# Four weighted slices in place of five plain ones for VectorE's share of the exponentials, with new scheduling constants, in an attention kernel

## The chip, the core and the metric

The kernel runs on one core of one Trainium2 chip. The metric is the device time of one execution, in microseconds (us). Each execution is marked fast or slow. A program on one core has no second core to compare with, but every execution used here is marked fast. Engines: PE is the matrix engine (TensorE), PEld its weight loads, ACT is ScalarE, DVE is VectorE, POOL is GpSimd, SP issues the DMAs.

The order of all instructions on every engine is fixed when the kernel is built: a scheduler written in Python, inside the kernel file, estimates times and places the work.

## The reference, cut to what matters

Two attentions over the same `x` (2048 tokens, width 640, 32 heads of 20) are mixed by a gate. A is full attention, with 32x2048x2048 exponentials. B is a dilated window of 8 keys, small in matmuls but large in elementwise work.

```python
scores = jnp.einsum("bhqd,bhkd->bhqk", q, k) * scale     # A: all pairs
p = _softmax(scores, axis=-1)
o = jnp.einsum("bhqk,bhkd->bhqd", p, v)
# B: keys at pos, pos-2, ..., pos-14 only
return g * a + (1 - g) * b
```

## The kernel before

A group is 512 queries of four heads. It has 64 score tiles (16 key blocks x 4 heads), each 128 keys x 512 queries in PSUM, and there are 32 groups: 2048 tiles. The scores are scaled so that 512 units are one octave.

ScalarE takes most tiles, two or three at a time:

```python
exps[s] = T("act", actc(512 * n), lambda e: e.activation(
    ebuf[s % NE][:, 0:512 * n], score[s % 2][:, 0:512 * n], ACTF.Exp, scale=LN2 / STEP), ...)
```

VectorE takes the rest in quads (one key block, four heads). A tile that it takes is called a ride. For each it moves the scores to 16-bit integers (an "eviction", `uD`). Then come the slices (`eD`), one per shift and quad. A slice computes `0.25*u + shift` as an int16 and lets PE read those bits as a bf16. That is a power of two with a straight line between octaves. The sum of several slices with different shifts smooths the line. The sum costs no addition, because PE accumulates P·V of every slice into the same bank:

```python
SHIFTS = (12001.875, 11976.375, 11952.625, 11935.625, 12034.125)
...
for k in range(K):                                   # gen_d
    T("dve", ..., lambda e, k=k, sl=sl: e.tensor_scalar(
        eD[:, sl % NS, 0:512 * n].bitcast(I16), uD[d % 2][:, 0:512 * n],
        0.25, SHIFTS[k], op0=ALU.mult, op1=ALU.add), ...)
```

The scheduler opens a quad when VectorE's backlog is small and the quad is far enough ahead of the end of its group (cuts marked):

```python
if idle < -DWAIT:                                    # VectorE too far behind
    return None
if not dopen:
    if ulock[...] or len(dquads) > cur["pv"] + 1 or ... or not (
            idle >= DIDLE2 or idle >= DIDLE and ...
            bdone[0] >= (now - BT0) / (BT1 - BT0) * BALL):    # B late: no quad
        return None
    ...  # and the quad must lie at least DTIME ahead
```

The padding (`filler`) issues matmuls that nobody reads wherever the plan leaves PE idle. At the end, the output projection of the last 512 rows (the "last fold") is prepared in `gen_prefold`; only the last group's share waits for `oN`.

## Time and profile before

| | before |
|---|---|
| time | 899.73 us median of 4 |
| ScalarE busy | 856.9 of 897.7 us |
| VectorE busy | 682.0 us |
| tiles of ScalarE / of VectorE | 1828 / 220 (55 quads) |
| exponential instructions | 726 |
| first exponential starts, last one ends | 21.3, 886.9 us |

The table of engines of the kernel before (busy time, share of the span, instructions):

```profile
span 897.7 us, 31434 instructions
PE 870.3 (97%) x13882; PEld 325.1 (36%) x13882; DVE 682.0 (76%) x1159; ACT 856.9 (95%) x760; POOL 79.2 (9%) x99
PE 75%; ACT 15%; DVE 5%; issue 3%; DMA 1%; SPq 0%; POOLq 0%; DVEq 0%; ACTq 0%; POOL 0%
```

The third line is the chain that ended last. It names PE, and so does the busy share, yet the groups of instructions argue against PE as the limit. Columns: line, engine, operation, output<-input, shapes, count | busy us, mean ns of one | idle us before them <- what ended it.

```profile
L1375 ACT ACTIVATE ebuf<-score 128x1536 bf16<-128x1536 f32 x377 | 525.4, 1477 | 7.9 <-PE score L1352 6.6 <-ACT ebuf L1375 0.3
L1375 ACT ACTIVATE ebuf<-score 128x1024 bf16<-128x1024 f32 x348 | 338.8, 1042 | 13.1 <-PE score L1352 11.1 <-PE score L487 0.3 <-PE side L844 0.2
...
L710 DVE TENSOR_SCALAR eD<-uD 128x2048 int16<-128x2048 uint16 x275 | 185.3, 703 | 20.2 <-PE obank L1410 19.6
L1365 DVE TENSOR_SCALAR uD<-score 128x512 uint16<-128x512 f32 x220 | 149.0, 687 | 57.7 <-PE score L1352 53.0 <-PE side L844 2.9
...
L1431 PE MATMUL score<-xT,ident 128*32 128x512 bf16 x1052 | 88.2, 381 | 0.1
L1431 PE MATMUL obank<-xT,zero 128*32 128x512 bf16 x1064 | 86.9, 383 | 0.1
```

ScalarE waits for only 21 us (7.9+13.1) in 865 us of exponentials. The last two lines, and a group of 120 more, are PE's padding: 2236 matmuls. The means overlap: 377x1.477+348x1.042 is 919 us, but the union is 841 us. The Trainium skill ("ScalarE: Activation LUTs", section "What ACT_TABLE_LOAD costs") gives 186 ns + 0.833 ns per element and an overlap of about 93 ns. The durations in this trace agree: 186+0.833x1024 = 1039 ns against 1042. The overlap is somewhat larger here: the durations of all 726 exponentials sum to 919.9 us, 78.5 us more than the union, which is 108 ns per step.

The end of the kernel before, ScalarE first, then PE (timeline: start us, us, engine, line, operation, count, idle before):

```profile
883.24 3.67 ACT L1375 ACTIVATE ebuf<-score 128x1536 bf16<-128x1536 f32 x3 [0.15 <-PE score L1352]
892.80 0.60 ACT L940 ACTIVATE stage<-side 128x512 bf16<-128x512 f32 x1 [5.90 <-PE side L921]
```

```profile
886.96 0.61 PE L1410 MATMUL obank<-ebuf,vA 128*21 128x512 bf16 x8 [0.75 <-ACT ebuf L1375]
887.40 1.25 PE L487 MATMUL side<-woBp,oB 128*32 128x512 bf16 x20
888.48 1.36 PE L487 MATMUL side<-woA_d,oTd 128*32 128x512 bf16 x20
889.77 1.26 PE L487 MATMUL score<-woBp,oB 128*32 128x512 bf16 x20
890.86 1.36 PE L487 MATMUL score<-woA_d,oTd 128*32 128x512 bf16 x20
892.15 0.40 PE L921 MATMUL score<-woA_l,oN 128*128 128x128 bf16 x4
```

The last P·V ends near 887.5. Then PE still does folds of two row blocks, though VectorE's last transposition, which makes `oN`, starts at 889.67, takes 0.71 us and is done at 890.4. The tail's own matmuls start at 892.15.

### The profile page before, as it was taken

The page shows a single profiled execution, that of the slowest core. Times are in us where ns is not written, and L with a number is a line of the kernel's source. Part 1 is how long each engine was busy: PE and PEld are TensorE (multiplying, and loading weights), DVE is VectorE, ACT ScalarE, POOL GpSimd, SP SyncE. Part 2 cuts the span into 40 slices and gives each one's busy share as a digit, 9 for nine tenths or more (in the row PEclk, how much of TensorE's full clock was granted, in tenths as well). Part 3 has the DMA queues.
Part 4 walks back from the last instruction along what each step waited for, and adds up shares of the span by engine and source line. Part 5 has one row for each costly group of instructions (what it writes and reads, how often), then busy time and mean ns, then how long its engine had stood idle before and what let it go on. Part 6 is the DMA issues. An engine that isn't in the chain of part 4 may idle for free.

```text
span 897.7 us, 31434 instructions
## 1 busy us (share of the span) xinstructions
PE 870.3 (97%) x13882; PEld 325.1 (36%) x13882; DVE 682.0 (76%) x1159; ACT 856.9 (95%) x760; POOL 79.2 (9%) x99
## 2 busy tenths in 40 slices
PE   8999998999999999999999999999999999999997
PEld 4433333433343333433333333433333333334333
DVE  6567779689788686878796887787888568778852
ACT  5999998999999999999999999999999999999995
POOL 5030007000000000000000000000000000000000
PEclk9999999999999999999999999999999999999999
DMA  9012112000011000000000001000000010000000
GB/s 295 24 40 44 40 29 77 16 16 13 13 27 27 21 17 21 14 19 6 19 17 24 9 12 26 14 19 5 13 10 19 20 35 10 5 5 6 6 5 32
DMA packets 34748, 24.00 MB, mean 27 GB/s; under 512 B 21684, under 2 KB 33412, under 8 KB 34612
## 3 DMA queue, kind: packets, MB, share of 16 engines
q1 hardware_dynamic: 34612, 21.99, 9.3%
q8 instruction: 109, 1.79, 0.8%
q14 instruction: 27, 0.22, 0.1%
HBM read 11.94 MB, written 2.62 MB: 16 GB/s over the span
## 4 chain that ended last, share of the span: by engine, by line
PE 75%; ACT 15%; DVE 5%; issue 3%; DMA 1%; SPq 0%; POOLq 0%; DVEq 0%; ACTq 0%; POOL 0%
PE score L1352 21%; PE side L487 18%; PE obank L1410 17%; ACT ebuf L1375 14%; PE obank L1431 6%; PE score L1431 5%; PE score L487 4%; DVE eD L710 1%; PE side L790 1%; DVE uD L1365 1%; DMA oTd<-in_A_x_dram 1%; PE side L844 1%; PE side L1431 1%; PE score L607 1%; DVE stage L777 1%
## 5 line engine op out<-in xcount | busy, mean ns | idle before, releaser
L1375 ACT ACTIVATE ebuf<-score 128x1024 bf16<-128x1024 f32 (+1 forms) x726 | 841.4, 1267 | 21.1 <-PE score L1352 17.7
L1352 PE MATMUL score<-qT,kT 32*128 32x512 bf16 x2048 | 287.6, 384 | 12.0 <-ACT ebuf L1375 8.4
L710 DVE TENSOR_SCALAR eD<-uD 128x2048 int16<-128x2048 uint16 x275 | 185.3, 703 | 20.2 <-PE obank L1410 19.6
L1365 DVE TENSOR_SCALAR uD<-score 128x512 uint16<-128x512 f32 x220 | 149.0, 687 | 57.7 <-PE score L1352 53.0
L1410 PE MATMUL obank<-ebuf,vA 128*21 128x512 bf16 x1828 | 164.9, 384 | 3.5 <-ACT ebuf L1375 2.2
L1352 PEld LDWEIGHTS score<-qT,kT 32*128 32x128 bf16 x2048 | 71.1, 91 | 258.1 <-issue 140.4
L487 PE MATMUL side<-xT,kvw 128*32 128x256 bf16 (+1 forms) x2520 | 99.1, 279 | 2.0 <-DVE qkvB L761 1.6
L1431 PE MATMUL score<-xT,ident 128*32 128x512 bf16 x1052 | 88.2, 381 | 0.1
L1410 PE MATMUL obank<-eD,vA 128*21 128x512 bf16 x1100 | 87.1, 379 | 0.0
L1431 PE MATMUL obank<-xT,zero 128*32 128x512 bf16 x1064 | 86.9, 383 | 0.1
L685 POOL TENSOR_TENSOR rcp<-rcp,gA 128x16 f32<-128x16 f32 x31 | 10.1, 325 | 777.4 <-DVE rcp L683 777.4
L487 PEld LDWEIGHTS side<-xT,kvw 128*32 128x32 bf16 x2520 | 60.0, 96 | 33.4 <-issue 13.5
L1410 PEld LDWEIGHTS obank<-ebuf,vA 128*21 128x21 bf16 x1828 | 39.2, 89 | 85.5 <-issue 65.3
L761 DVE CAST qkvB<-side 128x512 bf16<-128x512 f32 (+1 forms) x72 | 42.9, 595 | 13.4 <-PE side L487 13.1
L856 DVE TENSOR_TENSOR stage<-qkvB,repB 128x1280 bf16<-128x1280 bf16 x64 | 51.0, 824 | 0.7
L777 DVE TENSOR_TENSOR stage<-qkvB 128x1280 bf16<-128x1280 bf16 x64 | 51.2, 830 | 0.2
L487 PE MATMUL side<-stage,ident 128*32 128x512 bf16 (+1 forms) x768 | 47.9, 346 | 0.4 <-DVE outsb L965 0.4
L1431 PEld LDWEIGHTS obank<-xT,zero 128*32 128x32 bf16 x1064 | 24.0, 95 | 31.8 <-issue 20.7
L1431 PEld LDWEIGHTS score<-xT,ident 128*32 128x32 bf16 x1052 | 25.3, 95 | 28.1 <-ACT ebuf L1375 13.7
L1410 PEld LDWEIGHTS obank<-eD,vA 128*21 128x21 bf16 x1100 | 27.5, 92 | 20.6 <-issue 1.8
L690 POOL TENSOR_TENSOR oN<-oTt,rcp 128x512 bf16<-128x512 f32 x31 | 34.7, 1118 | 2.4
L679 DVE STREAM_TRANSPOSE oTt<-obank 128x512 f32<-128x512 f32 x32 | 22.8, 713 | 13.3 <-PE obank L1410 12.8
(155 smaller groups left out, 618.1 us busy)
## 6 DMA issues: line engine op xcount, KB each, us to landing
WqP<-in_A_wqkv_dram SPq DMA_DIRECT2D x16, 160.0 KB
stage<-in_B_wqkv_dram SPq DMA_DIRECT2D x1, 2400.0 KB
oTd<-oN SPq DMA_DIRECT2D x108, 20.0 KB
qT<-dst SPq DMA_DIRECT2D x104, 20.0 KB
out_dram<-outsb SPq DMA_DIRECT2D x12, 160.0 KB
kvw<-in_A_wqkv_dram SPq DMA_DIRECT2D x2, 800.0 KB
oTd<-in_A_x_dram SPq DMA_DIRECT2D x2, 640.0 KB
kT<-qkvB SPq DMA_DIRECT2D x14, 80.0 KB
```

What stands on the lines that cost most here:

```text
L487: ins = e.matmul(o[j:k, :], l[:, j:k], r, start=(first and i == 0), stop=(last and i == n - 1), skip_group_check=True)
L679: T("dve", dvc(512), lambda e: e.transpose(oTt[:, :], obank[:, :]), reads=["obank"], writes=["oTt"])
L690: T(en, c2, lambda e: e.tensor_tensor(oo, ii, ib, ALU.mult), reads=["rcp", "oTt"], writes=["oN0"])
L710: T("dve", 0.11 + 0.1334 * n, lambda e, k=k, sl=sl: e.tensor_scalar(eD[:, sl % NS, 0:512 * n].bitcast(I16), uD[d % 2][:, 0:512 * n], 0.25, ...
L761: t = TB(dvc(n * TOK), lambda e, o=o, i=i: e.tensor_copy(o, i), reads=[("side", b)], writes=[key])
L777: TB(dvc(CN * TOK, 2), lambda e, w=w, ks=ks: e.tensor_tensor(prodB(w), qB[:, :, :], ks, ALU.mult), reads=["qB", "kB"], writes=[("prod", w) ...
L856: TB(dvc(CN * TOK, 2), lambda e, w=w, vs=vs, rr=rr: e.tensor_tensor(prodB(w), vs, rr, ALU.mult), reads=["vB", ("repB", w4 % 2)], writes=[( ...
L1352: ins = e.matmul(o, kT[32 * j:32 * j + 32, q, kb * P:(kb + 1) * P], qT[g % NQT][32 * j:32 * j + 32, :], start=True, stop=True)
L1365: t = T("dve", 0.69, lambda e: e.tensor_scalar(uD[d % 2][:, 512 * i:512 * (i + 1)], side[x], UOFF, 0.0, op0=ALU.add, op1=ALU.max), reads=[ ...
L1375: exps[s] = T("act", actc(512 * n), lambda e: e.activation(ebuf[s % NE][:, 0:512 * n], score[s % 2][:, 0:512 * n], ACTF.Exp, scale=LN2 / S ...
L1410: ins = e.matmul(obank[32 * j:32 * j + DV, :], vA[:, kb, GROUPS[g][1], j, :], src, start=(kb == 0), stop=(last and k >= len(lst) - 4), ski ...
L1431: ins = e.matmul(o[32 * j:32 * j + 32, :], w[:, 32 * j:32 * j + 32] if best else w[:, :], xT[:, 0, 0:512], start=bool(best), stop=bool(bes ...
```

## The change

The intent: four slices with weights approximate the exponential as well as five plain ones. The weight is put on V, by three small GpSimd multiplies per quad, since P·V is linear. VectorE saves a slice per quad; the constants let it take more quads with that; side work that is late may use the other banks; the last fold has a higher priority. `woA_l` moves into a buffer that is used earlier for outputs.

```diff
-SHIFTS = (12001.875, 11976.375, 11952.625, 11935.625, 12034.125)
+SHIFTS = (12024.625, 12055.875, 12088.375, 12120.125)
+WEIGHTS = (1.0, 0.83984375, 0.71484375, 0.59375)
@@ gen_d
+        for k in range(1, K):
+            T("pool", 0.3, lambda e, k=k: e.tensor_scalar(
+                vS[:, d % 2, k - 1, :], _ap(vA, (kb * NQ + q) * 4 * DV, [[1, 4 * DV]]), WEIGHTS[k], None, op0=ALU.mult), ...)
@@ pv
+                v = vS[:, d % 2, k - 1, j * DV:(j + 1) * DV] if k else vA[:, kb, GROUPS[g][1], j, :]
@@ the rule for banks 1 and 2 (called "the bank rule" below)
-            if best and not force and (ent[0] > XPRIO or ...
+            if best and not force and (ent[0] > xprio() or ...
+    def xprio():
+        return XPRIO if bdone[0] >= (sch.avail["pe"] - XT0) / (XT1 - XT0) * BALL else XLATE
@@ the constants
-    DTIME = 17.0
+    DTIME = 14.0
-    BT1 = 820.0
+    BT1 = 900.0
-    DWAIT = 0.6
+    DWAIT = 1.0
@@ the last fold
-                    add_gen(gen_prefold(), 5.5)
+                    add_gen(gen_prefold(), 2.2)
+                    add_gen(gen_prefold2(), 2.3)
+                    add_gen(gen_wl(), 2.4)
(cut: woA_l in outsb[0] and its late load; gen_prefold split in two; the new bank rule also in crowded())
```

A calculation on paper (all integer inputs of four octaves, rounding to the nearest integer assumed) gives a ripple of 0.098% rms for the five plain slices and 0.114% for the four weighted ones.

More of the change, by code (lines that the diff above doesn't have):

```diff
@@ L284, in _build @@
     woA_d = sb([P, CN, D], BF16, "woA_d")
-    woA_l = sb([P, D], BF16, "woA_l")
     woBp = sb([P, CN, D], BF16, "woBp")
@@ L329, in _build @@
     oB = sb([P, CN, 512], BF16, "oB")
+    vS = sb([P, 2, K - 1, 4 * DV], BF16, "vS")
     kst = [qkvB[:, 0:S], _ap(oB, 0, [[1, S]])]
     outsb = [sb([P, D], BF16, "outsb%d" % i) for i in range(2)]
+    woA_l = outsb[0]
     idf = rB[:, 0:P]
@@ L440, in constants @@
             yield ("cond",)
-        T("sp", 5.0, lambda e: [e.dma_start(woA_l[32 * j + 1:32 * j + 1 + DH, :], A_wo[j * DH:(j + 1) * DH, :])
-                                for j in range(4)], writes=["woA_l"], dma=True, nd=4)
         T("sp", 5.0, lambda e: [e.dma_start(woA_d[o:o + m, c, :], A_wo[d:d + m, :])
@@ L704, in gen_d @@
             yield ("cond",)
+        g, kb = dquads[d]
+        q = GROUPS[g][1]
+        while cur["pv"] < d - 1 or not done.get(("v", kb, q // 4)):
+            yield ("cond",)
+        for k in range(1, K):
+            T("pool", 0.3, lambda e, k=k: e.tensor_scalar(
+                vS[:, d % 2, k - 1, :], _ap(vA, (kb * NQ + q) * 4 * DV, [[1, 4 * DV]]), WEIGHTS[k], None, op0=ALU.mult),
+              reads=[("vA", kb, q // 4), "vAones"], writes=[("vS", d % 2, k)])
         for k in range(K):
@@ L903, in gen_prefold, with gen_wl, gen_prefold2 @@
             release(b, t)
-        while not d_over():
+        done["prefold1"] = True
+    WL = [("outsb", 0, 0), ("outsb", 0, 1)]
+    def gen_wl():
+        while not all(done.get(("fold", QCN - 2, hu)) for hu in range(2)):
             yield ("cond",)
+        T("pool", 0.8, lambda e: e.memset(woA_l[:, :].bitcast(FP32), 0.0), writes=WL)
+        T("sp", 5.0, lambda e: [e.dma_start(woA_l[32 * j + 1:32 * j + 1 + DH, :], A_wo[j * DH:(j + 1) * DH, :])
+                                for j in range(4)], writes=WL, dma=True, nd=4)
+    def gen_prefold2():
+        while not (done.get("prefold1") and d_over()):
+            yield ("cond",)
+        rd = [("oTd", (QCN - 1) % 2, q) for q in range(1, NQ)] + ["woA_d", "woBp"] + [
+            ("oB", hu, f0) for hu in range(2) for f0 in range(0, CN, 2)]
+        qs = None
         for blk in range(2):
@@ L915, in tail @@
         q = [NQ - 1]
-        rd = ["oN1", "woA_l"]
+        rd = ["oN1"] + WL
         def mm(key, lst, accum):
@@ L1010, in step @@
                 return False
-            if best and not force and (ent[0] > XPRIO or any(o_[3][0] == "pe" and o_[3][2] <= now + 0.3 for o_ in gens)):
+            if best and not force and (ent[0] > xprio() or any(o_[3][0] == "pe" and o_[3][2] <= now + 0.3 for o_ in gens)):
                 return False
@@ L1027, in _build @@
     XPRIO = 2.5
+    XLATE = 6.6
+    XT0 = 150.0
+    XT1 = 880.0
+    def xprio():
+        return XPRIO if bdone[0] >= (sch.avail["pe"] - XT0) / (XT1 - XT0) * BALL else XLATE
     def order():
@@ L1143, in _build @@
             kT[:, q, :].bitcast(FP32), _ap(ones2, 0, [[0, S // 2], [1, 2]]).bitcast(FP32)), reads=["ones2"], writes=[("kTz", q)])
-    T("pool", 0.8, lambda e: e.memset(woA_l[:, :].bitcast(FP32), 0.0), writes=["woA_l"])
     turned(1)
@@ L1334, in crowded @@
     def crowded(x):
-        return sum(bank_used) == 1 and any(ent[3][0] == "bank" and ent[0] <= XPRIO for ent in gens) and bank_free[x] <= min(
+        return sum(bank_used) == 1 and any(ent[3][0] == "bank" and ent[0] <= xprio() for ent in gens) and bank_free[x] <= min(
             [bank_free[b] for b in range(NB) if not bank_used[b]])
@@ L1388, in pv @@
             rd.add(("ebuf", s % NE))
-            lst.append((g, r // 4, r % 4, ebuf[s % NE][:, i * 512:(i + 1) * 512]))
+            kb, j = r // 4, r % 4
+            lst.append((g, kb, j, vA[:, kb, GROUPS[g][1], j, :], ebuf[s % NE][:, i * 512:(i + 1) * 512]))
             left_a[g] -= 1
@@ L1394, in pv @@
             rd.add(("eD", sl))
+            if k:
+                rd.add(("vS", d % 2, k))
             for i, j in enumerate(ridden[d]):
-                lst.append((g, kb, j, eD[:, sl, 512 * i:512 * (i + 1)]))
+                v = vS[:, d % 2, k - 1, j * DV:(j + 1) * DV] if k else vA[:, kb, GROUPS[g][1], j, :]
+                lst.append((g, kb, j, v, eD[:, sl, 512 * i:512 * (i + 1)]))
             left_d[g] -= len(ridden[d])
             npv[0] += 1
-        for g, kb, j, _ in lst:
+        for g, kb, j, _, _ in lst:
             if not done.get(("v", kb, (GROUPS[g][1]) // 4)):
@@ L1408, in fn @@
             ins = None
-            for k, (g, kb, j, src) in enumerate(lst):
-                ins = e.matmul(obank[32 * j:32 * j + DV, :], vA[:, kb, GROUPS[g][1], j, :], src,
+            for k, (g, kb, j, v, src) in enumerate(lst):
+                ins = e.matmul(obank[32 * j:32 * j + DV, :], v, src,
                                start=(kb == 0), stop=(last and k >= len(lst) - 4), skip_group_check=True)
```

## The prediction

> **What bounds the kernel.** ScalarE. The engine table gives ACT 856.9 of 897.7 us; the groups by form give 377 exponentials of 128x1536 (1477 ns) and 348 of 128x1024 (1042 ns), with 21 us of idle time before them. The rest is a start of 21 us and a tail (timeline) from the last exponential, 886.9 us, to the end, 10.8 us. PE is 97% busy, but 2236 of its matmuls (`ident` and `zero` with xT) are padding: PE has room.
>
> VectorE takes 220 of the 2048 tiles (55 quads): a 687 ns eviction per tile and five 703 ns slices per quad. A quad costs DVE 4x0.687+5x0.703 = 6.26 us, 344 of its 682 busy us. A tile that DVE takes turns a 1536 exponential into a 1024 one: 0.435 us of ACT, 1.74 us per quad.
>
> **What the change does.**
> 1. Four slices instead of five. A quad costs DVE 5.56 us; with 55 quads DVE would lose 38.7 us and PE 220 matmuls, about 12 us of its time. None of that is on the chain. It pays only if the scheduler takes more quads. It will: fewer slices free the two quad buffers earlier, the allowed DVE backlog rises (0.6 to 1.0), the minimum lead falls (17 to 14), and B's schedule runs to 900 instead of 820, so that B is less often "late" and holds back fewer quads. The windows show the room: 16 evictions per 50 us between 200 and 350 us, but 11 to 12 in most stretches after 550 us.
>    Estimate: 64 quads (60 to 69). DVE then needs 338+64x5.56 = 694 us, about today's. ACT saves 9x1.74 = 15.7 us.
> 2. GpSimd gets three 128x84 multiplies per quad, about 190. From its 16-element (221 ns) and 400-element (520 ns) operations I estimate 0.28 us each, 54 us on an engine busy for 79. Little waits for them: slice 0 uses plain V. But they read SBUF. The Trainium skill, "SBUF — State Buffer", section "Who interferes with whom", says that a VectorE instruction in a 2-port mode and a GpSimd one exclude each other for the whole instruction, as do a two-input VectorE one and a reading GpSimd one. This trace agrees: slices take 683 ns with no GpSimd work beside them (261), and up to 1829 ns beside the GpSimd copies. The multiplies are short, and slices plus two-input products cover about 28% of the time. Estimate: 5 to 15 us of extra DVE time, at most a third of the saving; 0 to 4 us on the chain.
> 3. The last fold. In the timeline PE runs the first two blocks' fold matmuls from 887.4 to 892.1 us, after the last P·V and in front of the tail's own, though oN is ready at 890.4. With a higher priority they run earlier: about 1.7 us off the tail. The late load of `woA_l` should be hidden.
>
> Sum: 900 - 15.7 - 1.7 + 2 = 885 us, range 873 to 896; faster by over 2% 0.41, within 2% 0.55, slower 0.04.
>
> **What would show it.** About 256 evictions and 256 slices; ACT exponential time about 825 us; DVE busy 680 to 720 us; GpSimd busy 130 us or more; some slices lengthened to about 1 us; no `woBp` matmuls after the last P·V; last exponential to end about 9 us.
>
> **What would make it wrong.** If quads stay near 57, little but the tail is won (about 895). If locks make DVE late against the static order, PE, which runs in order, waits for slices or evictions, and ACT's idle time exceeds 30 us. With DVE at 85% and 70 quads, about 873. If B slips to the end, the last fold is exposed and the tail grows.

## More of the kernel before

The kernel's lists do not change while it runs. So a change of a scheduling constant makes another list, and a list has counts (tiles, exponentials, quads) that can be read before it runs.

A ride uses a third PSUM bank that would otherwise hold a third tile of the exponential. So do B's matmuls and other side work when they are allowed in that bank. In both cases the exponential has two tiles instead of three.

## The result and the profile after

| | before | after |
|---|---|---|
| time, median of 4 | 899.73 us | 886.81 us (885.85 to 888.85) |
| ratio | | 0.986 (0.984 to 0.988) |
| quads | 55 | 66 |
| exponential instructions | 726 | 789 |
| VectorE busy | 682.0 us | 699.8 us |
| last exponential ends | 886.9 us | 875.4 us |
| from there to the end | 10.7 us | 11.6 us |

Ratios here and below are the mean time of one kernel's fast runs over that of the other's fast runs of the same rounds, so they are not quite the ratio of the medians. The profile is of the slowest of the four runs (888.85 us). The interval is clear of 1: the kernel is 1.4% faster.

The table of engines, then groups of instructions, of the kernel after, with the same columns as before:

```profile
span 887.1 us, 30664 instructions
PE 863.4 (97%) x13206; PEld 309.5 (35%) x13206; DVE 699.8 (79%) x1192; ACT 845.0 (95%) x823; POOL 212.4 (24%) x297
```

```profile
L1403 ACT ACTIVATE ebuf<-score 128x1024 bf16<-128x1024 f32 x581 | 557.4, 1037 | 15.6 <-PE score L1380 12.8 <-ACT ebuf L1403 0.2
L1403 ACT ACTIVATE ebuf<-score 128x1536 bf16<-128x1536 f32 x207 | 292.5, 1469 | 5.7 <-PE score L1380 4.6 <-ACT ebuf L1403 0.3
...
L718 DVE TENSOR_SCALAR eD<-uD 128x2048 int16<-128x2048 uint16 x264 | 179.1, 702 | 13.1 <-PE obank L1442 12.4
L1393 DVE TENSOR_SCALAR uD<-score 128x512 uint16<-128x512 f32 x264 | 178.2, 684 | 58.2 <-PE score L1380 55.5
...
L710 POOL TENSOR_SCALAR vS<-vA 128x84 bf16<-128x84 bf16 x198 | 130.8, 665 | 120.0 <-PE obank L1442 111.4
```

The first two lines hold the result. There are 233 more two-tile exponentials than before and 170 fewer of three. Only 264 of the 581 have a ride; 317 have two tiles because the third bank was in use by something else (before: 348-220 = 128). So 44 fewer tiles save 18.8 us by the fit, 63 more instructions cost 5.4 us, and together with 1.5 us that the fit does not explain the exponentials fell from 841.4 to 829.5 us, by 11.9. The idle time of ScalarE hardly changed (21.1 to 21.7 us), and the tail grew by 0.9 us. So the two profiled spans differ by 10.6 us. The medians differ by 12.9 us, because the profiled run of after is its slowest, 2 us above its median. It holds a stretch of 3.4 us at half the granted clock at 222 us, which the profiles of no_multiply and old_fold below, in all but the same order, do not have; their idle time is 19.0 and 19.1 us.

The end of the kernel after, ScalarE and PE:

```profile
874.85 0.60 ACT L1403 ACTIVATE ebuf<-score 128x512 bf16<-128x512 f32 x1 [0.52 <-PE score L1380]
882.19 1.09 ACT L963 ACTIVATE stage<-score 128x512 bf16<-128x512 f32 x2 [6.74 <-PE score L944]
```

```profile
875.50 0.40 PE L1442 MATMUL obank<-ebuf,vA 128*21 128x512 bf16 x4 [0.47 <-ACT ebuf L1403]
...
876.77 1.26 PE L487 MATMUL score<-woBp,oB 128*32 128x512 bf16 x20
877.86 1.36 PE L487 MATMUL score<-woA_d,oTd 128*32 128x512 bf16 x20
879.15 1.26 PE L487 MATMUL score<-woBp,oB 128*32 128x512 bf16 x20
880.24 1.36 PE L487 MATMUL score<-woA_d,oTd 128*32 128x512 bf16 x20
881.54 1.26 PE L944 MATMUL score<-outsb,oN 128*128 128x128 bf16 x8
```

The same two row blocks are still folded after the last P·V, behind 44 small matmuls of the fold (cut above), and the pause on ScalarE is 6.74 us instead of 5.90. The fold's new order won nothing here.

### The profile page after: what moved, and what is told of

It reads as the page before. It is cut to its first block, busy times and chain, and to the rows that moved or that the text cites. A ratio compares the mean times of both kernels' runs of the same rounds, so it can differ in the third digit from the quotient of the medians.

```text
span 887.1 us, 30664 instructions
## 1 busy us (share of the span) xinstructions
PE 863.4 (97%) x13206; PEld 309.5 (35%) x13206; DVE 699.8 (79%) x1192; ACT 845.0 (95%) x823; POOL 212.4 (24%) x297
## 4 chain that ended last, share of the span: by engine, by line
PE 68%; ACT 21%; issue 5%; DVE 3%; POOL 2%; DMA 0%; SPq 0%; DVEq 0%; ACTq 0%; POOLq 0%
PE score L1380 21%; ACT ebuf L1403 20%; PE obank L1442 15%; PE side L487 12%; PE score L487 11%; PE obank L1463 3%; PE score L1463 2%; PE side L1463 1%; POOL kvw L732 1%; POOL vS L710 1%; DVE oTt L679 0%; DVE stage L785 0%; PE obank L393 0%; PE score L1097 0%; PE side L852 0%
## 5 line engine op out<-in xcount | busy, mean ns | idle before, releaser
L1403 ACT ACTIVATE ebuf<-score 128x1024 bf16<-128x1024 f32 (+1 forms) x789 | 829.5, 1150 | 21.7 <-PE score L1380 17.9
L1380 PE MATMUL score<-qT,kT 32*128 32x512 bf16 x2048 | 314.7, 384 | 9.5 <-ACT ebuf L1403 5.0
L1393 DVE TENSOR_SCALAR uD<-score 128x512 uint16<-128x512 f32 x264 | 178.2, 684 | 58.2 <-PE score L1380 55.5
L718 DVE TENSOR_SCALAR eD<-uD 128x2048 int16<-128x2048 uint16 x264 | 179.1, 702 | 13.1 <-PE obank L1442 12.4
L710 POOL TENSOR_SCALAR vS<-vA 128x84 bf16<-128x84 bf16 x198 | 130.8, 665 | 120.0 <-PE obank L1442 111.4
L685 POOL TENSOR_TENSOR rcp<-rcp,gA 128x16 f32<-128x16 f32 x31 | 12.5, 402 | 501.6 <-DVE rcp L683 501.6
L1442 PE MATMUL obank<-eD,vS 128*21 128x512 bf16 x792 | 69.6, 382 | 0.0
L487 PE MATMUL score<-xT,kvw 128*32 128x256 bf16 (+2 forms) x1310 | 66.0, 295 | 0.0
L487 PE MATMUL side<-xT,kvw 128*32 128x256 bf16 (+1 forms) x1450 | 63.1, 284 | 0.4 <-DVE qkvB L769 0.3
L1463 PE MATMUL obank<-xT,zero 128*32 128x512 bf16 x756 | 63.2, 383 | 0.0
L1463 PE MATMUL score<-xT,ident 128*32 128x512 bf16 x572 | 47.9, 381 | 0.1
L487 PEld LDWEIGHTS side<-xT,kvw 128*32 128x32 bf16 x1450 | 34.0, 96 | 21.2 <-issue 13.6
L487 PEld LDWEIGHTS score<-xT,kvw 128*32 128x32 bf16 (+1 forms) x1310 | 30.8, 95 | 22.4 <-issue 15.9
```

Of the source, the lines that this page charges most:

```text
L487: ins = e.matmul(o[j:k, :], l[:, j:k], r, start=(first and i == 0), stop=(last and i == n - 1), skip_group_check=True)
L710: T("pool", 0.3, lambda e, k=k: e.tensor_scalar(vS[:, d % 2, k - 1, :], _ap(vA, (kb * NQ + q) * 4 * DV, [[1, 4 * DV]]), WEIGHTS[k], None, ...
L718: T("dve", 0.11 + 0.1334 * n, lambda e, k=k, sl=sl: e.tensor_scalar(eD[:, sl % NS, 0:512 * n].bitcast(I16), uD[d % 2][:, 0:512 * n], 0.25, ...
L1380: ins = e.matmul(o, kT[32 * j:32 * j + 32, q, kb * P:(kb + 1) * P], qT[g % NQT][32 * j:32 * j + 32, :], start=True, stop=True)
L1393: t = T("dve", 0.69, lambda e: e.tensor_scalar(uD[d % 2][:, 512 * i:512 * (i + 1)], side[x], UOFF, 0.0, op0=ALU.add, op1=ALU.max), reads=[ ...
L1403: exps[s] = T("act", actc(512 * n), lambda e: e.activation(ebuf[s % NE][:, 0:512 * n], score[s % 2][:, 0:512 * n], ACTF.Exp, scale=LN2 / S ...
```

## The experiments

Twelve kernels were run in timed rounds beside the kernel before. All passed the comparison with the reference; how little that says of the slices' accuracy is told under `no_multiply`. "Instr." are the exponentials in the kernel's lists (a profile can miss a record). "Busy" and "idle" are of the exponentials' group line, "tail" is from the last exponential's end to the end of the span (from the timeline).

| kernel | slices | quads | instr. | busy | idle | tail | time | ratio to before (95%) |
|---|---|---|---|---|---|---|---|---|
| before | 5 | 55 | 726 | 841.4 | 21.1 | 10.7 | 899.0 to 899.7 | 1 |
| after | 4 | 66 | 789 | 829.5 | 21.7 | 11.6 | 886.8 | 0.986 (0.984 to 0.988) |
| slices_only | 4 | 58 | 723 | 837.2 | 21.5 | 10.3 | 895.3 | 0.995 (0.994 to 0.997) |
| rest_only | 5 | 63 | 798 | 836.7 | 32.0 | 11.6 | 906.7 | 1.008 (1.006 to 1.009) |
| no_xlate | 4 | 64 | 725 | 824.7 | 19.5 | 34.4 | 902.5 | 1.004 (1.002 to 1.005) |
| no_multiply | 4 | 66 | 789 | 829.0 | 19.0 | 11.6 | 885.5 | 0.985 (0.983 to 0.986) |
| old_constants | 4 | 57 | 746 | 840.6 | 21.5 | 9.3 | 897.1 | 0.997 (0.995 to 0.999) |
| old_fold | 4 | 66 | 788 | 829.0 | 19.1 | 12.0 | 885.5 | 0.985 (0.983 to 0.986) |
| extra_vector | 4 | 66 | 789 | 833.6 | 27.3 | 11.6 | 897.9 | 0.998 (0.997 to 1.000) |
| five_retuned | 5 | 63 | 793 | 836.3 | 23.8 | 12.6 | 897.9 | 0.998 (0.997 to 1.000) |
| three_same | 3 | 75 | 807 | 817.8 | 22.4 | 25.0 | 891.1 | 0.990 (0.989 to 0.992) |
| three_slices | 3 | 75 | 758 | 811.1 | 21.3 | 15.9 | 874.7 | 0.973 (0.971 to 0.974) |
| two_slices | 2 | 81 | 775 | 804.5 | 18.2 | 14.6 | 862.8 | 0.959 (0.958 to 0.961) |
| no_padding | 4 | 66 | 784 | 829.8 | 44.3 | 12.5 | 914.5 | 1.016 (1.012 to 1.020) |

Theory: the time is ScalarE's ledger, start + busy + idle + tail, where busy follows from the tiles and instructions in the list. Slices, constants and the bank rule matter through that count and through what they leave late. Rivals: the freed VectorE time brings the gain by itself; the constants bring it; the port lock between GpSimd and VectorE eats it; PE is the limit.

### slices_only: the slices alone

```diff
-    DTIME = 14.0 / BT1 = 900.0 / DWAIT = 1.0 / XLATE = 6.6
+    DTIME = 17.0 / BT1 = 820.0 / DWAIT = 0.6 / XLATE = 2.5    # XLATE = XPRIO: the old bank rule
-    add_gen(gen_prefold(), 2.2); add_gen(gen_prefold2(), 2.3)
+    add_gen(gen_prefold(), 5.5); add_gen(gen_prefold2(), 5.5)
```

> Four weighted slices and the GpSimd multiplies, with the scheduling constants, the bank rule and the fold priorities of before. Its instruction lists hold 58 quads and 723 exponentials (before: 55 and 726). Theory (ScalarE's own time decides: 0.427 us per tile plus 0.085 us per instruction, fitted to the two profiles): 1816 tiles and 723 instructions take 836 us against 841 before, so about 895 us. Rival (the freed VectorE and TensorE time brings the gain by itself): 887 us, as the whole change.

Measured: 895.31 us, as the ledger said, and a third of the gain. VectorE's busy time fell to 667.1 us and ScalarE's idle time stayed at 21.5 us. The freed time did nothing by itself that these numbers show; three more quads account for the gain. The first rival falls.

```profile
L1403 ACT ACTIVATE ebuf<-score 128x1024 bf16<-128x1024 f32 (+1 forms) x723 | 837.2, 1257 | 21.5 <-PE score L1380 17.3 <-ACT ebuf L1403 0.3 <-PE side L824 0.3
```

### rest_only: everything but the slices

```diff
-SHIFTS = (12024.625, 12055.875, 12088.375, 12120.125)
+SHIFTS = (12001.875, 11976.375, 11952.625, 11935.625, 12034.125)
(the GpSimd multiplies taken out; every slice multiplies with plain V)
```

> The five plain slices of before with every other part of the change (constants, bank rule, fold order, late load). Its lists hold 63 quads and 798 exponentials. Theory: 1796 tiles and 798 instructions take 834 us of ScalarE, 7 us less than before; VectorE then needs 338+63x6.26 = 732 us and is late more often, so 892 to 897 us. Rival (the constants alone bring the gain, the slices nothing): 887 us or less.

Measured: 906.7 us, slower than before and a miss of the theory's range. The exponentials' group line of this kernel:

```profile
L1397 ACT ACTIVATE ebuf<-score 128x1024 bf16<-128x1024 f32 (+1 forms) x797 | 836.7, 1148 | 32.0 <-PE score L1374 27.6 <-PE side L485 0.3 <-ACT ebuf L1397 0.3
```

Busy is 836.7 us (the fit had said 834), so that part held. What was added is idle time, 32.0 us, nearly all of it spent waiting for scores from PE. Of the 32.0 us, 5.0 lie inside a stretch of 10 us at half the granted clock that starts at 157.5 us; the other 27.0 us are still 6 us more than before. The mean clock is 0.994 to 0.996 in all four runs, so the stretch probably belongs to this kernel and not to one run. So the rest of the change does not bring the gain alone; it costs 7 to 8 us.

### no_xlate: without the bank rule

```diff
-    XLATE = 6.6
+    XLATE = 2.5
```

> The changed kernel without the rule that lets late B work take the score banks. Its lists hold 64 quads and 725 exponentials (after: 66 and 789). If the number of tiles and of exponential instructions alone decided, ScalarE would need 826 us, 3 us less than after, and the time would be 884 us. Theory: the rule is there so that B ends in time; without it B's last windows and the folds come after the last exponential, the time from the last exponential to the end grows from 12 to more than 20 us, and the kernel takes 895 to 910 us.

Measured: 902.5 us. Busy was the lower, at 824.7 us (fit 826.2), and the kernel was still 16 us slower than after. Its group of exponentials, and its last ScalarE lines (timeline):

```profile
L1403 ACT ACTIVATE ebuf<-score 128x1024 bf16<-128x1024 f32 (+1 forms) x724 | 824.7, 1253 | 19.5 <-PE score L1380 17.1 <-PE side L852 0.3
...
864.96 2.84 ACT L1403 ACTIVATE ebuf<-score 128x1536 bf16<-128x1536 f32 x2
897.27 0.60 ACT L963 ACTIVATE stage<-side 128x512 bf16<-128x512 f32 x1 [29.48 <-PE side L944]
```

ScalarE has nothing to do for 29.5 us. B's last combination on VectorE starts at 883.4 us here and at 853.0 us in after, and the last fold needs it. So most of the 317 two-tile exponentials without a ride (380-256 = 124 in this trace, 128 before) are the price for B in time, and here the price is worth paying.

### no_multiply: what the GpSimd multiplies cost

The edit, in short and not word for word:

```diff
-                vS[:, d % 2, k - 1, :] = WEIGHTS[k] * V      # tensor_scalar on GpSimd, 128x84
+                vS[:, d % 2, k - 1, 0:1] = 0                 # memset, one element; P·V reads plain V
```

> The changed kernel in the same static order, but each GpSimd multiply is a memset of one element per partition and all slices use plain V: a wrong result on purpose (four plain slices sum to about 1.3 times their share). It measures what the multiplies cost through the shared SBUF port and through the waits on them. Theory: the slices' mean falls from 702 to about 690 ns, and the time by 0 to 2 us (885 to 887 us). Rival (the lock makes VectorE late and TensorE waits): 880 us or less.

Measured: 885.45 us against 886.8 in another session; the ratios 0.985 and 0.986 have overlapping intervals, so at most about 1.4 us. VectorE's slices, in the group line of this kernel (after: 179.1 us, mean 702; the expectation said about 690):

```profile
L718 DVE TENSOR_SCALAR eD<-uD 128x2048 int16<-128x2048 uint16 x264 | 177.6, 697 | 13.3 <-PE obank L1442 12.5
```

All VectorE work together is 1.8 us shorter (698.0 against 699.8). The lock is there, but GpSimd pays for it: in after its multiplies last 0.42 us at the median and 0.665 us in the mean, up to 3.8 us. The 120 that stay under 0.5 us have slices or two-input VectorE work beside them for 0.03 us on average; the 78 longer ones, 1.04 us in the mean, for 0.90 us. Nobody on the chain waits for them long (PE 5.5 us in 18 waits). The third rival falls.

This kernel leaves the weights out, and it still passed the comparison. A calculation of A's output in floating point, for eight heads and 512 queries with two of the sixteen key blocks approximated, gives an error of 10.6% for it, 0.11% for the four weighted slices, 0.12% for the five plain ones and 0.11% for exact exponentials rounded to bf16. So "correct" does not test the slices. A reworking from the reference's inputs gave about 10% for no_multiply and 0.10 to 0.20% for the others, depending on the offset assumed for the scores. It also shows a limit: these inputs' scores spread by only about 3 units (standard deviation) of the 512 in an octave, so the calculation samples a small piece of the curve. For scores that spread over octaves the ripple is the figure to look at.

### old_constants: four slices and the bank rule with the old constants

```diff
-    DTIME = 14.0 / BT1 = 900.0 / DWAIT = 1.0
+    DTIME = 17.0 / BT1 = 820.0 / DWAIT = 0.6
```

> The changed kernel with the three constants of before (minimum lead 17, B's schedule to 820, allowed backlog 0.6); four slices, bank rule and fold order of after. Its lists hold 57 quads and 746 exponentials. Theory: 1820 tiles and 746 instructions take 840 us of ScalarE, 2 us less than before, and the tail stays near 11 us: 897 to 899 us, so worse than the slices alone (895.3), because the bank rule splits exponentials and no quads pay for it. Rival (the constants hardly matter): 887 us.

Measured: 897.05 us, within the range and 1.7 us worse than the slices alone (the intervals of the two ratios overlap). The bank rule splits exponentials (746 instructions against 723), and without more quads nothing pays for it. Its tail, 9.3 us, shows that the last fold can be further along when the exponentials end.

### old_fold: the fold at its old priority

```diff
-    add_gen(gen_prefold(), 2.2); add_gen(gen_prefold2(), 2.3)
+    add_gen(gen_prefold(), 5.5); add_gen(gen_prefold2(), 5.5)
```

> The changed kernel with the fold's generators at the priority of before (5.5). Its lists hold 66 quads and 788 exponentials, as after. Theory: the last fold starts when the second to last group has landed, and TensorE has no more free time in front of the last exponential whatever the priority; the tail stays within 1 us of 11.6 us and the time within 1 us of 886.8. Rival (the new order takes time off the tail, as predicted): 1.5 to 2 us slower.

Measured: 885.47 us, tail 12.0 us. It is no slower than after (ratios 0.985 and 0.986); the time is 0.3 us below the expected band. The priority of the fold is worth nothing that these runs can see.

### extra_vector: VectorE loaded again, in the same order

```diff
+                if k == 0:
+                    e.tensor_reduce(spare[:, 0:1], uD[d % 2][:, 0:512], AX.X, ALU.max)   # before each quad's first slice
```

> The changed kernel in the same static order with one more VectorE operation per quad in front of its first slice: a maximum over 128x512 of the quad's values into an unused cell, 66 of about 0.68 us, 45 us in all, so VectorE is loaded as with five slices and 66 quads; the result stays right. Theory: the order is fixed with VectorE's time in mind, so the extra time makes evictions and slices late, TensorE waits for them and ScalarE's idle time grows from 21 us to 30 us or more: 893 to 903 us. Rival (VectorE is idle for 187 us and absorbs it): 888 us or less.

Measured: 897.9 us, 11 us slower. The expectation of 30 us of idle time was a little high; the line says 27.3:

```profile
L1409 ACT ACTIVATE ebuf<-score 128x1024 bf16<-128x1024 f32 (+1 forms) x789 | 833.6, 1148 | 27.3 <-PE score L1386 22.7 <-ACT ebuf L1409 0.4
```

Idle time is 5.6 us more than in after. Busy is 4.1 us more with the same exponentials, and the trace shows why. Their durations sum to 905.6 us (after: 907.0), so as a whole they did not become longer; but 158 of them start after the one before has ended, against 126 in after. An exponential that starts late loses the overlap, and the loss is counted as busy time. Over all fourteen profiles the fit's error follows the number of such late starts, from -1.5 us at 93 to 5.4 us at 158, by about 0.1 us each (correlation 0.96). The 35 that became late in this kernel lost 3.5 us of overlap. So most of these 4.1 us too are lateness. PE waits longer for evictions before it writes scores (29.5 us in 67 waits; after 20.6 in 49). VectorE was idle for 187 us in after, and yet a quarter of the 45 us of added operations came out at the end (they overlap others, so VectorE's busy time rose by 34.9 us). In this fixed order, VectorE's time costs although no view calls VectorE the limit.

### five_retuned: five slices with constants of their own

```diff
 (as rest_only)
-    DTIME = 14.0 / DIDLE = -1.0 / BT1 = 900.0 / XT1 = 880.0
+    DTIME = 13.0 / DIDLE = -1.5 / BT1 = 860.0 / XT1 = 900.0
```

> Five plain slices with every other part of the change, and constants chosen anew for five slices out of 500 random sets (minimum lead 13, B's schedule to 860 for the quads and to 900 for the banks, threshold of idle -1.5). Its lists hold 63 quads and 793 exponentials. Theory: the bad result of rest_only was five slices under constants made for four; 1796 tiles and 793 instructions take 834 us of ScalarE, 8 us less than before, so 890 to 894 us. Rival (63 quads are too many for VectorE with five slices): above 900 us.

Measured: 897.9 us. Better than rest_only by 9 us, so part of that result was constants that did not suit five slices. It is above the theory's range, though: busy 836.3 (fit 833.7), idle 2.7 us and tail 1.9 us more than before. It has the same stretch of 10 us at half clock near 158 us, and again 5.0 us of ScalarE's idle time lie inside it. Five slices won 0.2% this way, at the edge of what the interval can tell from nothing. A better set of constants may exist, but 500 sets tried by the plan gave none.

### three_same and three_slices: one slice fewer

```diff
-SHIFTS = (12024.625, 12055.875, 12088.375, 12120.125)
-WEIGHTS = (1.0, 0.83984375, 0.71484375, 0.59375)
+SHIFTS = (12076.625, 12118.875, 12162.125)
+WEIGHTS = (1.0, 0.80078125, 0.63671875)
(three_slices only:)
-    DTIME = 14.0 / DIDLE = -1.0 / XT0 = 150.0 / XT1 = 880.0
+    DTIME = 15.0 / DIDLE = -0.5 / XT0 = 200.0 / XT1 = 860.0
```

The constants of three_slices, two_slices and five_retuned were chosen among random sets (500 for five_retuned) by the scheduler's own plan, which ranks orders but gives no time that is used here.

> Three weighted slices with the constants of the change untouched. Its lists hold 75 quads and 807 exponentials. If tiles and instructions alone decided: 1748 and 807 take 814.5 us of ScalarE, 14 us less than after, so 873 us. Theory: constants made for four slices let the quads crowd out B, whose last products and folds then come after the last exponential: the tail grows beyond 20 us and the kernel takes 880 to 892 us.

> The changed kernel with three weighted slices (ripple of the approximated exponential 0.21% rms by calculation, against 0.10% for the five plain and 0.11% for the four weighted) and retuned constants (minimum lead 15, threshold of idle -0.5, B from 200 to 860). Its lists hold 75 quads and 758 exponentials. Theory: 1748 tiles and 758 instructions take 810 us of ScalarE, 31 us less than before, so 868 to 871 us, clear of both kernels. Rival (VectorE, with 338+75x4.87 = 703 us, is late, or TensorE is at its end): 878 us or more, with ScalarE's idle time above 30 us.

Measured: 891.1 and 874.7 us with the same 75 quads. In three_same the exponentials end at 864.3 us, but then ScalarE waits (timeline):

```profile
884.47 0.60 ACT L963 ACTIVATE stage<-side 128x512 bf16<-128x512 f32 x1 [20.13 <-PE score L944]
```

B's last combination starts at 868.3 us, after the exponentials. With other constants the same number of quads left a tail of 15.9 us and 49 fewer exponential instructions. The theory's 868 to 871 us for three_slices was missed by 4 us: the busy time was right (811.1, expected 810), and the tail was 15.9 us, where that range leaves room for about 11.

### two_slices: two slices, the best version

```diff
+SHIFTS = (12152.375, 12216.875)
+WEIGHTS = (1.0, 0.70703125)
+    DTIME = 9.0 / DIDLE = -1.5 / BT1 = 840.0 / DWAIT = 0.6 / XT0 = 200.0 / XT1 = 840.0
```

> The same with two weighted slices (ripple 0.45% rms by calculation) and its own constants (minimum lead 9, backlog 0.6, threshold of idle -1.5, B from 200 to 840). Its lists hold 81 quads and 775 exponentials. Theory: 1724 tiles and 775 instructions take 801 us of ScalarE, 40 us less than before: 859 to 863 us. Rival (as for three slices): 872 us or more.

Measured: 862.83 us (862.2 to 864.24), 4.1% faster than before and clear of both kernels. Its exponentials:

```profile
L1403 ACT ACTIVATE ebuf<-score 128x1024 bf16<-128x1024 f32 x601 | 578.5, 1038 | 16.5 <-PE score L1380 12.0 <-PE obank L1442 0.5 <-ACT ebuf L1403 0.3
L1403 ACT ACTIVATE ebuf<-score 128x1536 bf16<-128x1536 f32 x174 | 248.0, 1470 | 1.7 <-PE score L1380 1.4
```

VectorE is busy for 679.7 us, as before, with 81 quads instead of 55. That the time met the range is partly luck: busy time was 3.5 us above the expectation and the tail 4 us longer than before, while idle time was 3 us shorter.

The calculation of the output error named above gives 0.14% for two weighted slices and 0.18% for three, close to the 0.11% of exact exponentials in bf16; the reworking gave 0.11 to 0.20% for two and 0.11 to 0.17% for three. The chip's comparison could not have told, so the accuracy rests on such calculations for these inputs. The ripple is 0.45% rms against 0.098% of the five plain slices, so for wider scores the two kernels are not equally accurate.

### no_padding: is PE the limit?

```diff
-    FILL = 0.85
+    FILL = 0.0
```

> The changed kernel without the 1648 padding matmuls (threshold of the filler 0). Its lists hold 66 quads and 784 exponentials (after: 789). Theory: TensorE has room, the padding runs in time that nothing waits for, and only keeps the granted clock up; without it TensorE's busy share falls from 97% to about 85%, ScalarE's idle time stays within 4 us of 21 us if the clock stays at 1.0, and the time within 4 us of 886.8. If the clock falls below 0.97, the time rises above 895 us. Rival (TensorE, with 68% of the chain, is the limit, and the padding stands in front of real work): 5 us or more faster.

Measured: 914.5 us (909 to 916), with a mean granted clock of 0.937. The four runs lie between 0.937 and 0.946. Page lines, first the clock in 40 slices (in tenths), then the exponentials' group:

```profile
PEclk9999999978999999999989979799989999889579
```

```profile
L1403 ACT ACTIVATE ebuf<-score 128x1024 bf16<-128x1024 f32 (+1 forms) x784 | 829.8, 1163 | 44.3 <-PE score L1380 41.6 <-ACT ebuf L1403 0.2
```

Taking away 1648 useless matmuls made the kernel 28 us slower. They do not stand in front of real work; they keep the clock up. Without them the trace has 16 stretches of 3.4 to 20.5 us at half clock (the last at the very end, where before has one too), and PE is busy for 90% of the span, where the expectation said about 85%. The mean of one score matmul rises from 384 to 404 ns, and ScalarE waits 22.6 us longer. Of its 44.3 us of idle time 22.9 lie inside the stretches; outside them 21.4 are left, as many as after has in all. The list is not quite the same (784 exponentials against 789), but the fit puts that at 0.4 us. The rival that PE is the limit falls in the form that was tested, but the theory's "room" was half true: the time is free, the activity is not.

## Why the prediction was right or wrong

The total was right: 885 us predicted, 886.8 measured. That it came so near is partly luck, because terms that were off cancelled in part: 15.7 + 1.7 - 2 = 15.4 us of gain predicted, 12.9 measured. Two quads more than predicted came, the lock cost less, the bank rule cost what nobody had counted, and the tail grew.

1. **More quads, through the constants**: right. Predicted 64 (60 to 69), measured 66. slices_only has 58 and old_constants 57, so neither the slices nor the bank rule makes the quads; the constants do, and four slices make them affordable: with five, rest_only and five_retuned end at 906.7 and 897.9 us.
2. **"ACT saves 9x1.74 = 15.7 us"**: the mis-sized term. With the 11 quads that came it would have been 19.1 us; the exponentials saved 11.9. The step that failed is that a ride only turns one three-tile exponential into a two-tile one and leaves the rest alone. The bank rule gave the third bank to B far more often: 317 two-tile exponentials without a ride against 128, 63 instructions more in all, 5.4 us. The prediction did not cost the bank rule at all. no_xlate shows both sides: with 64 quads and no bank rule the exponentials take 824.7 us, where the prediction said 825 for 64 quads; but the tail is then 34.4 us.
3. **"None of that is on the chain"** (VectorE's freed time): too strong. slices_only agrees with it, since freeing VectorE alone brought no less idle time. But extra_vector shows that the reverse costs: 45 us more VectorE work in the same order made the kernel 11 us slower. So it is likely, though not shown by itself, that the saved slice also kept 66 quads from being late.
4. **The lock**: mechanism right, sizes wrong. Predicted 5 to 15 us of extra VectorE time, measured 1.8 us; predicted 0 to 4 us on the chain, measured at most about 1.4. The multiply was estimated at 0.28 us and took 0.42 us at the median. GpSimd waited for VectorE far more than the other way round.
5. **The last fold, "about 1.7 us off the tail"**: wrong, in sign. The tail grew from 10.7 to 11.6 us, and old_fold shows the priority to be without effect. In after the fold's first matmuls start at 860.5 us, 8.4 us after the second to last group's transposition on VectorE starts (before: 8.3 us, 862.3 to 870.6). From there to the last P·V PE runs no padding and is idle for 0.4 us. So what stood in the way was when they could start, not their rank. From that start to the last exponential's end there are 14.9 us in after, 16.3 before and 17.1 in old_constants, and the tails, 11.6, 10.7 and 9.3 us, go the other way.
6. **"PE has room"**: right in that nothing waits behind the padding, incomplete in that the padding holds the clock (no_padding, 28 us).

What stays open: why the two five-slice kernels with the bank rule have one 10 us stretch at half clock near 157 us and after has none there (one of 3.4 us, at 222 us); what brings the 27.0 us of rest_only's idle time that lie outside that stretch; and what two plain slices with shifts of their own would have done.

## What to carry to other kernels

Before crediting an offload with the time that it takes from the bounding engine, count that engine's instructions too: tiles x time per element plus instructions x fixed cost gave the busy time of every variant here to within 3.4 us of 805 to 841, except extra_vector (5.4 us), and what it missed followed the number of late starts. Follow a saved resource to what spends it: here a cheaper slice was worth 4 us by itself and 13 us with constants that spent it, while constants and bank rule without it lost 8, or won about 1.6 with constants of their own. And when an approximation has a linear operand behind it, as V is here, weights can go onto that operand. They lower the ripple of a given number of slices (0.45% for two, where the best two plain ones that a search found have 0.54%), but a further slice lowers it more (0.21% for three weighted, 0.25% for three plain). The 4.1% of two_slices comes with fewer slices and more quads; two plain slices were not run, and no_multiply, where the multiplies cost at most about 1.4 us, suggests that they would take about the same time.

## What the Trainium skill lacked or had wrong

- "TensorE: Matmul & The Clock Gate", section "HAM oscillation — how this bites in real kernels", puts the rule as no idle gaps of PE above about 3.4 us. In no_padding PE's longest idle time after the start was 1.5 us (busy for 90% of the span), and the clock still fell to half in 16 stretches, 0.937 on average, at a cost of 28 us. So that rule is not enough. The section after it ("A second HAM failure mode: psum-queue depth-cycling") does name frequent short idle times as a cause, as here; what the page lacks is a figure for how much activity holds the clock.
- "SBUF — State Buffer", section "Who interferes with whom", is right about the lock (slices of 683 ns took up to 1829 ns beside GpSimd copies). That section does not say that a blocked instruction's wait appears inside its recorded duration: the multiplies show 413 to 3802 ns for the same 128x84 work, so of their 130.8 us of busy time only about 83 (198x0.42) are work.
- "GPSIMD Engine Reference", section 3.1, has a time for a 2048-element operation and a cost per element, but no fixed cost of a short one. A one-input multiply of 128x84 bf16 took 0.42 us here.
- "ScalarE: Activation LUTs", section "What ACT_TABLE_LOAD costs", was nearly right: 186+0.833N ns less about 93 ns of overlap, that is 93 ns per instruction in a row, against 85 ns fitted here, where the overlap averages 98 ns (after) to 108 ns (before) per step. It would have been better to count instructions with it in the prediction than to use means of the table alone.
